# The last tile of a spectral filter, its buffers, its issue order, and the first row blocks behind it

## The chip, the cores and the metric

The kernel runs on one NeuronCore of one Trainium2 chip. The metric is the device time of one execution in microseconds (us); the smaller it is the better. The engines are named as the profile names them: PE (matrix multiply), PEld (its weight loads), DVE (VectorE), ACT (ScalarE), POOL (GpSimd) and SP, which here does nothing but issue DMAs.

## What is computed

A layer of two residual branches on x, 2048 rows of 512 float32 values:

```
h  = x + irfft2( rfft2(layernorm(x)) * (w_r + 1j*w_i) )
h2 = h + ( gelu(layernorm(h) @ w_gate) * (layernorm(h) @ w_up) ) @ w_down
```

w_gate and w_up are 512x1376, w_down is 1376x512. All outputs are float32.

## The kernel before

The Fourier transforms are matrix multiplications, folded by symmetry. **First stage**: 16 row blocks of 128 rows are transformed along the rows. **Filter stage** (the loop over `SECOND`): 16 tiles t. For each, `over_d` (L411) transforms along d (matmul L416, copied by ACT, L420), and `filtered` (L422) finishes the forward transform on PE (L427), multiplies by the weights on DVE (three products, L433 to L435, into t1 and t2) and adds z = t1 + t2 (L438) with a two-column patch behind it (L440): on POOL for tiles 0 to 14, on DVE for tile 15. `back` (L442) takes z back on PE (L448, two halves e of two matmuls each) and ACT copies the bank into gh (L450). z has 7 buffers. A tile is written into all 16 row blocks of gh, so no row block can be begun before the last tile is copied.

**Row blocks** (the list `FIRST`): for block b, `U` takes it back along d with four matmuls (`over_d_back`, L510, matmul L515), `C` copies the bank by ACT (L830), `V` adds its halves on DVE (L838) and `X` subtracts them on POOL (L866) into the two halves of one row `v`, `M` multiplies `v` by `mis` on PE (L848), `O`, `H`, `G` and `I` undo the symmetry and add x; the rest of the list normalizes the blocks and begins the gated layer. The remaining time, some 300 us, is the gated layer on PE.

The weights of the gated layer are split into a rounded part and a rest by `load_gu`: a weight tile lands in `raw`, **which has one buffer**; POOL makes sums of it (L138 to L146); then, for the first two weight tiles, seven pairs follow of a rounding on ACT (L93) and a subtraction on POOL (L94). The generator is advanced by one step at each `h` in `SECOND`; the steps cover weight tiles 0 and 1. In `FIRST`, `r0` is the first POOL step (L138) of weight tile 2, whose DMA into `raw` (L131, L132) can start when the last L94 of weight tile 1 has read the buffer.

Both lists are written out by hand, and the engines PE, ACT, DVE and POOL get their instructions in the order of the lists; each engine works strictly in its order. In `SECOND`, `o3.0` is `over_d` of tile 3 into bank 0, `f3` is `filtered`, `b3` is `back`, `p3` patches the weights of tile 3 on ACT (L453), and `h` is a step of the weight split. The loads of x for row blocks 0, 1, 4 and 5 go into `a` (L783), memory that the filter stage's buffers held before; SP too works in order.

Of the kernel before, what the change touches and what calls it, by code (L numbers as in the profile page):

```python
# [12 lines left out]
F32 = mybir.dt.float32  # L13
F32R = mybir.dt.float32r
I32 = mybir.dt.int32
AF = mybir.ActivationFunctionType
ALU = mybir.AluOpType
# [3 lines left out]
P = 128  # L21
NB = 16
NT = 16
NF = 11
NQ = 260
# [6 lines left out]
BY_THEN = (8, 12, 9)  # L32

FIRST = """
U4.0 C4.0 r0 U0.1 C0.1 U1.2 U5.3 V4.2 X4 V0.3 C1.4 V1.0 C5.5 X0 M4.1 V5.1 X1 O4.0 X5 M0.2 H4 U2.3 O0.1 G4 I4
M5.1 C2.5 H0 V2.3 G0 S4 U7.2 M1.3 O5.0 A4 U6.0 I0 U3.4 X2 H5 C7.1 S0 O1.1 A0 H1 M2.1 C6.0 Q0 C3.5 E0.5 N0 G5
U12.3 R01 V7.4 I5 T01.2 G1 I1 V6.3 S5 X7 A5 R00 T00 S1 O2.1 M7.0 X6 s0.0 A1 a0 Q1 l0 V3.1 E1.6 c0 d0 f0 b0 U8.4
U9.7 N1 e0.1 m0 g0 H2 h0 R10 k0 T10 R11 H7 n0 T11.1 X3 a1 s1.2 b1 c1 i0 d1 j0 l1 M3.2 C8 S7 g0aP0 o0 M6.4 e1.0
# [8 lines left out]
"""  # L47

SECOND = """
p0 p1 p2 h o0.0 h o1.6 o2.2 f0 o3.0 f1 p3 o4.2 f2 p4 h o5.0 o6.2 h f3 o7.0 h h p5 h f4 o8.2 p6 f5 b0 p7 b1 f6 o9.2 h h  # L50
h f7 p8 p9 b2 b3 o10.2 p10 f8 b4 h p11 o11.2 p12 f9 b5 o12.2 h h f10 b6 f11 o13.2 p13 b7 f12 h h o14.2 b8 f13 p14 o15.2
h f14 p15 b9 b10 h f15 b11 h b12 b13 b14 b15
"""
AHEAD = 8

# [2 lines left out]
def kernel(  # L58
# [16 lines left out]
    pe, act, dve, pool = nc.tensor, nc.scalar, nc.vector, nc.gpsimd  # L75
    x3 = x.rearrange("(p b) d -> p b d", b=NB)
    o3 = out.rearrange("(p b) d -> p b d", b=NB)

    base = ctx.enter_context(tc.tile_pool(name="base", bufs=1))
    gh = base.tile([P, NB, D], F32, name="gh")  # L80
# [25 lines left out]
    ps = ctx.enter_context(tc.tile_pool(name="ps", bufs=1, space=PSUM)).tile([P, 8, 512], F32, name="ps")  # L106
# [55 lines left out]
    with (  # L162
# [245 lines left out]
        w2 = ctx2.enter_context(tc.tile_pool(name="w2", bufs=2, reuse_waits="tile"))  # L408
        dps, zs = {}, {}
# [12 lines left out]
        def filtered(t):  # L422
            dp, wt = dps.pop(t), wts.pop(t)
            px = ps[:, 4 + 2 * (t % 2) : 6 + 2 * (t % 2), :NQ]
            for g in range(2):
                r = dp[:, g].rearrange("p e q -> p (e q)")
                pe.matmul(px[:, g], cfs[:, min(t, 1), g], r, start=True, stop=True)  # L427

            t1 = w2.tile([P, 2, NQ], F32, name="t1", bufs=3)
            t2 = w2.tile([P, 2, NQ], F32, name="t2", bufs=3)  # L430
            z = w2.tile([P, 2, NQ], F32, name="z", bufs=7)
            re, im = slice(0, 64), slice(64, P)
            dve.tensor_tensor(t1, px, wt[:, 0], op=ALU.mult)  # L433
            dve.scalar_tensor_tensor(t2[re], px[im], -1.0, wt[im, 1], op0=ALU.mult, op1=ALU.mult)
            dve.tensor_tensor(t2[im], px[re], wt[re, 1], op=ALU.mult)  # L435

            eng = dve if t == NT - 1 else pool
            eng.tensor_tensor(z, t1, t2, op=ALU.add)  # L438
            zs[t] = z
            eng.tensor_tensor(z[:, :, 0], z[:, :, 0], z[:, :, 128], op=ALU.add)  # L440

        def back(t):  # L442
            z = zs.pop(t)
            pg = ps[:, t % 2].rearrange("p (c g n) -> p c g n", c=4, g=2)
            for e in range(2):
                for g in range(2):
                    o, zg = pg[:, 2 * e : 2 * e + 2, g], z[:, g, 130 * e : 130 * e + P]
                    pe.matmul(o, zg, cis[:, min(t, 1), g], start=True, stop=True)  # L448
            ghv = gh.rearrange("p b (c t k) -> p t c b k", c=8, k=4)[:, t]
            act.activation(ghv, ps[:, t % 2].rearrange("p (c b k) -> p c b k", c=8, k=4), AF.Copy)  # L450

        def patch_w(t):
            act.activation(wts[t][:, :, :, 0:129:128], wh[:, t], AF.Copy)  # L453
# [2 lines left out]
        with tc.manual_schedule(engines={et.PE, et.Activation, et.DVE, et.Pool}):  # L456
            prep = itertools.chain(raw0, load_gu(1, True))
            for m, op in enumerate((ALU.add, ALU.subtract)):
                pool.tensor_tensor(wh[:, :, m], ws[:, 0, :, m], ws[:, 1, :, m], op=op)
            with tc.issue_after(kept.ins):  # L460
                act.activation(wh, wh, AF.Copy, scale=0.5)
            for _ in range(4):
                next(prep)
            rounded = 0
            for op in SECOND.split():
                name, *place = op.split(".")
                t = int(name[1:] or 0)
                if name == "h":
                    for _ in range(2 if rounded == 6 else 1):
                        next(prep, None)  # L470
                    rounded += 1
                elif name[0] == "o":
                    over_d(t, int(place[0]))
                elif name[0] == "f":
                    filtered(t)
                    if t + AHEAD < NT:
                        load_w(t + AHEAD)
                    if t == NT - 1:
                        for k, b in enumerate(BY_PE):
                            act.activation(nis[:, k], mis[:, b], AF.Copy, scale=-1.0)  # L480
                else:
                    (patch_w if name[0] == "p" else back)(t)
# [19 lines left out]
    def stats2(b):  # L502

        bn = w3.tile([P, 32], F32, name="bn")[:, :6]
        dve.bn_stats(bn, gh[:, b])
        yield
        dve.bn_aggr(mv2[:, b], bn)
        yield

    def over_d_back(b, bank):  # L510

        g = gh[:, b].rearrange("p (c k) -> p c k", c=4)
        pv = ps[:, bank].rearrange("p (e s n) -> p e s n", e=2, s=2)
        for c in range(4):
            pe.matmul(pv[:, c // 2, (c + c // 2) % 2], g[:, c], dis[:, c], start=True, stop=True)  # L515

    def norm_scales(b, n):
# [269 lines left out]
    do = {}  # L787
# [5 lines left out]
    def early(b):  # L793

        where = []

        def back(k):
            where.append(k)
            over_d_back(b, k)

        do[f"U{b}"] = back
        do[f"C{b}"] = lambda: act.activation(gh[:, b], ps[:, where[0]], AF.Copy)
        do[f"K{b}"] = lambda k: unfolded(b, rows[k])
# [9 lines left out]

    def whole(b):

        pv = sv = v = py = od = None
        xt, by_pe = sources[b], b in BY_PE

        def parts(a):
            return a.rearrange("p (e s n) -> p e s n", e=2, s=2)  # L820

        def back(k):
            nonlocal pv
            pv = ps[:, k]
            over_d_back(b, k)

        def keep(k):
            nonlocal sv
            sv = parts(rows[k])
            act.activation(rows[k], pv, AF.Copy)  # L830

        def unfold(k):
            nonlocal v
            v = rows[k]
            if b in BY_POOL:
                pool.tensor_tensor(parts(v)[:, :, 0], sv[:, :, 0], sv[:, :, 1], op=ALU.add)
            else:
                dve.tensor_tensor(parts(v)[:, :, 0], parts(pv)[:, :, 0], sv[:, :, 1], op=ALU.add)  # L838

        def back_s(k):  # L840
            nonlocal py
            py = ps[:, k].rearrange("p (e n) -> p e n", e=2)
            if by_pe:
                for e, m in enumerate((mis[:, b], nis[:, BY_PE.index(b)])):
                    pe.matmul(py[:, e], mis[:, b], v[:, :256], start=True, stop=False)
                    pe.matmul(py[:, e], m, v[:, 256:], start=False, stop=True)
            else:
                pe.matmul(ps[:, k], mis[:, b], v, start=True, stop=True)  # L848

        def odd(k):  # L850
            nonlocal od
            od = ods[k]
            act.activation(od, py[:, 1], AF.Copy)

        def residual():
            x2 = xt.rearrange("p (e n) -> p e n", e=2)
            y = py if by_pe else py[:, 0:1].to_broadcast([P, 2, 256])
            to = gh[:, b].rearrange("p (e n) -> p e n", e=2) if by_pe else x2
            dve.scalar_tensor_tensor(to, x2, mv[:, b, 0:1], y, op0=ALU.subtract, op1=ALU.add)

        def unfold2(e, op):
            x2, h2 = (a.rearrange("p (e n) -> p e n", e=2) for a in (xt, gh[:, b]))
            return lambda: pool.tensor_tensor(h2[:, e], x2[:, e], od, op=op)

        do[f"U{b}"], do[f"C{b}"], do[f"V{b}"], do[f"M{b}"] = back, keep, unfold, back_s
        do[f"X{b}"] = lambda: pool.tensor_tensor(parts(v)[:, :, 1], sv[:, :, 0], sv[:, :, 1], op=ALU.subtract)  # L866
        do[f"O{b}"], do[f"H{b}"] = odd, residual
        do[f"G{b}"], do[f"I{b}"] = unfold2(0, ALU.add), unfold2(1, ALU.subtract)
        st = stats2(b)
        do[f"S{b}"] = do[f"A{b}"] = lambda: next(st)  # L870
# [43 lines left out]
    for b in range(8):  # L914
        whole(b)
# [62 lines left out]
    with tc.manual_schedule(engines={et.PE}):  # L978
        for n, (q, f) in list(enumerate(tiles))[2:]:
            k, at_change = n - q * NF, n == NF - 1  # L980
# [175 lines left out]
```

## Time and profile before

| | us |
|---|---|
| median of 3 runs | 457.14 (456.63 to 457.20) |
| profiled execution, whole | 456.41 |
| profiled execution, span of the profile | 454.6 |
| PE busy | 438.9 (97% of the span) |
| first stage ends, filter stage begins (first L416) | 33.43 |
| last tile's copy (L450) ends, row blocks begin (first L515) | 78.06 |
| first M (L848) begins | 81.74 |

The profile is of one execution; its instructions carry source lines, so the stages can be told apart by line. The time line gives start and duration of each instruction or run of equal instructions; the chain of waits follows the end of the program back from each instruction to what released it. A busy PE says little alone: what counts are the places where it is idle and what ended that idle time.

### The profile page before, as it was taken

To read this page: it belongs to the slowest core of one execution; us is meant where nothing else is said; L and a number is where in the kernel's file an instruction comes from. 1 tells how busy PE (TensorE), PEld (TensorE's weight loads), DVE (VectorE), ACT (ScalarE), POOL (GpSimd) and SP (SyncE) were. 2 spreads that over 40 slices of the span, in tenths; PEclk is the share of its full clock that TensorE was granted. 3 is DMA by queue.
4 is the path that set the end of the run, shared out by engine and by line. 5 is a ranking of instruction groups with operands and counts; after the bars stand their busy time and mean duration, and the time that the engine had idled before them with its cause. 6 is when DMAs were issued, how large, how long until landed. Compare 5 with 4: busy or idle time off the path is not lost.

```text
span 454.6 us, 6435 instructions
## 1 busy us (share of the span) xinstructions
PE 438.9 (97%) x2289; PEld 371.4 (82%) x2289; DVE 276.9 (61%) x513; ACT 206.6 (45%) x433; POOL 275.5 (61%) x305
## 2 busy tenths in 40 slices
PE   3999998999999999999999999999999999999997
PEld 3899998788967777887888888888888888888876
DVE  5966986797665676358744579256565355535453
ACT  3979876688751233024422776242243024302420
POOL 5985996968868578828752744155566536663210
PEclk9999999999999999999999999999999999999999
DMA  8994804300031122112210203131022102210013
GB/s 253 399 406 132 284 32 156 123 25 1 25 115 47 48 92 92 48 47 71 69 46 25 70 25 128 57 85 55 25 70 69 48 24 71 69 46 25 23 66 121
DMA packets 21168, 41.05 MB, mean 90 GB/s; under 512 B 2064, under 2 KB 7696, under 8 KB 21008
## 3 DMA queue, kind: packets, MB, share of 16 engines
q1 hardware_dynamic: 21136, 40.64, 26.2%
q8 instruction: 18, 0.29, 0.3%
q14 instruction: 14, 0.11, 0.1%
HBM read 36.44 MB, written 4.19 MB: 89 GB/s over the span
## 4 chain that ended last, share of the span: by engine, by line
PE 89%; ACT 4%; DVE 2%; DMA 2%; issue 1%; SPq 1%; DVEq 0%; ACTq 0%
PE ps L747 26%; PE ps L100 15%; PE ps L102 15%; PE ps L101 15%; PE ps L416 3%; PE ps L515 3%; PE ps L427 3%; PE ps L448 2%; PE ps L288 2%; DMA gh<-in_x 2%; PE ps L848 1%; PE ps L956 1%; PE ps L554 1%; ACT ts L293 1%; PE ps L548 1%
## 5 line engine op out<-in xcount | busy, mean ns | idle before, releaser
L100 PE MATMUL ps<-cb,gu 128*128 128x512 f32 (+1 forms) x336 | 127.8, 380 | 2.0 <-ACT s L651 1.6
L747 PE MATMUL ps<-wd,a 128*128 128x512 f32 (+1 forms) x537 | 126.1, 388 | 0.2 <-DVE gh L750 0.2
L102 PE MATMUL ps<-cb,gu 128*128 128x512 f32 (+1 forms) x336 | 124.9, 372 | 0.0
L101 PE MATMUL ps<-cb,gu 128*128 128x512 f32 (+1 forms) x336 | 124.8, 371 | 0.0
L747 PEld LDWEIGHTS ps<-wd,a 128*128 128x128 f32 x537 | 99.2, 188 | 22.4 <-DVE gh L957 0.9
L156 POOL TENSOR_TENSOR gu<-raw,gu 128x768 fp32r<-128x768 f32 (+1 forms) x54 | 78.2, 1476 | 40.0 <-DVE gu L153 38.7
L651 ACT ACTIVATE s<-ps 128x512 f32<-128x512 f32 (+1 forms) x72 | 40.4, 561 | 134.4 <-PE ps L102 134.2
L100 PEld LDWEIGHTS ps<-cb,gu 128*128 128x128 f32 x336 | 63.2, 188 | 15.0 <-ACT s L651 2.2
L101 PEld LDWEIGHTS ps<-cb,gu 128*128 128x128 f32 x336 | 63.2, 188 | 11.7 <-issue 1.0
L102 PEld LDWEIGHTS ps<-cb,gu 128*128 128x128 f32 x336 | 63.2, 188 | 11.1
L753 DVE TENSOR_TENSOR gh<-ps,gh 128x512 f32<-128x512 f32 x48 | 33.0, 690 | 53.5 <-PE ps L747 53.4
L496 POOL TENSOR_TENSOR wd<-wdr,wd 128x512 fp32r<-128x512 f32 x22 | 28.5, 1295 | 51.5 <-ACT wd L494 51.5
L660 DVE TENSOR_TENSOR ps<-ps,s 128x512 f32<-128x512 f32 (+1 forms) x48 | 31.0, 649 | 24.8 <-PE ps L102 22.5
L666 ACT ACTIVATE a<-ps 128x512 fp32r<-128x512 f32 (+1 forms) x48 | 26.9, 561 | 39.0 <-DVE ps L660 38.6
L673 DVE TENSOR_TENSOR a<-ps,a 128x512 fp32r<-128x512 f32 (+1 forms) x48 | 30.7, 640 | 11.8 <-ACT a L666 10.4
L138 POOL TENSOR_TENSOR raw<-raw 128x256 f32<-128x256 f32 x20 | 14.7, 737 | 37.8 <-DMA raw<-in_wgu 36.7
L654 DVE TENSOR_TENSOR s<-ps,s 128x512 f32<-128x512 f32 (+1 forms) x48 | 30.8, 642 | 10.3 <-PE ps L102 8.7
L657 ACT ACTIVATE s<-s 128x512 f32<-128x512 f32 (+1 forms) x48 | 28.2, 592 | 18.4 <-DVE s L654 18.4
L654 DVE TENSOR_TENSOR ps<-ps,s 128x512 f32<-128x512 f32 (+1 forms) x24 | 15.7, 654 | 27.7 <-ACT s L651 27.7
L288 PE MATMUL ps<-ms,pn 128*128 128x128 f32 x120 | 17.6, 297 | 8.3 <-ACT ms L256 8.1
L288 PEld LDWEIGHTS ps<-ms,pn 128*128 128x128 f32 x120 | 16.1, 210 | 8.8 <-POOL pn L263 8.8
L153 DVE CAST gu<-raw 128x1792 fp32r<-128x1792 f32 x18 | 19.6, 1091 | 4.5 <-PE ps L101 2.9
(124 smaller groups left out, 609.7 us busy)
## 6 DMA issues: line engine op xcount, KB each, us to landing
raw<-in_wgu SPq DMA_DIRECT2D x40, 256.0 KB, 3.1
wt<-in_w SPq DMA_DIRECT2D x16, 520.0 KB, 5.4
wdr<-in_wd SPq DMA_DIRECT2D x22, 256.0 KB, 2.6
out<-gh SPq DMA_DIRECT2D x15, 256.0 KB, 2.0
gh<-in_x SPq DMA_DIRECT2D x7, 512.0 KB, 9.6
row<-in_x SPq DMA_DIRECT2D x12, 256.0 KB, 3.0
mis<-in_mi SPq DMA_DIRECT2D x1, 1024.0 KB, 10.7
a<-in_x SPq DMA_DIRECT2D x4, 256.0 KB, 4.3
```

The lines of the kernel that those rows point to most:

```text
L100: pe.matmul(o, lh, rh, start=(i == 0 and not onto), stop=False, skip_group_check=True)
L101: pe.matmul(o, lh, rl, start=False, stop=False, skip_group_check=True)
L102: last = pe.matmul(o, ll, rh, start=False, stop=(i == n - 1), skip_group_check=True)
L156: pooled["lo"] = pool.tensor_tensor(r[:, 1, m], t[:, m], r[:, 0, m].bitcast(F32), op=ALU.subtract)
L288: pe.matmul(pt[:, c], o, mc, start=(z == 0), stop=(z == len(parts[b][c]) - 1))
L496: pool.tensor_tensor(r[:, 1], t, r[:, 0].bitcast(F32), op=ALU.subtract)
L651: return lambda: act.activation(to, a, AF.Copy)
L654: return lambda: dve.tensor_tensor(to, a, b, op=ALU.add)
L660: return lambda: dve.tensor_tensor(u, u, g, op=ALU.mult)
L673: dve.tensor_tensor(a[:, 1], u, a[:, 0].bitcast(F32), op=ALU.subtract)
L747: pe.matmul(o, parts_of[tiles.index((q, f))][:, ha, i // 4, r], wds[f][:, hw, c], start=start, stop=stop)
L753: dve.tensor_tensor(gh[:, b, c], o, gh[:, b, c], op=ALU.add)
```

## The change

Four things are changed. (1) The sum z of tile 15 is split by columns: DVE adds columns 0 to 129 of each half and patches them, POOL adds columns 130 to 259. (2) The copy of tile 15 into gh is split: the matmuls of its second half e write bank 3, ACT copies the first half, DVE the second. (3) z gets 14 buffers. (4) `SECOND` is in a new order, and `FIRST` begins row blocks 4 and 0 by halves of d: `u4` and `u0` do the two matmuls that need the first half of gh, `w4` and `w0` the other two.

```diff
 FIRST = """
-U4.0 C4.0 r0 U0.1 C0.1 U1.2 U5.3 V4.2 X4 V0.3 C1.4 V1.0 C5.5 X0 M4.1 V5.1 X1 O4.0 X5 M0.2 H4 U2.3 O0.1 G4 I4
+u4.0 u0.1 w4 C4.0 r0 w0 C0.1 U1.2 U5.3 V4.2 X4 V0.3 C1.4 V1.0 C5.5 X0 M4.1 V5.1 X1 O4.0 X5 M0.2 H4 U2.3 O0.1 G4 I4
...
 SECOND = """
...
-h f14 p15 b9 b10 h f15 b11 h b12 b13 b14 b15
+f14 p15 h b9 b10 f15 h h b11 b12 h b13 b14 h b15
...
-            z = w2.tile([P, 2, NQ], F32, name="z", bufs=7)
+            z = w2.tile([P, 2, NQ], F32, name="z", bufs=14)
...
+            zs[t] = z
+            first = slice(0, NQ)
+            if t == NT - 1:
+                first, second = slice(0, 130), slice(130, NQ)
+                pool.tensor_tensor(z[:, :, second], t1[:, :, second], t2[:, :, second], op=ALU.add)
             eng = dve if t == NT - 1 else pool
-            eng.tensor_tensor(z, t1, t2, op=ALU.add)
-            zs[t] = z
+            eng.tensor_tensor(z[:, :, first], t1[:, :, first], t2[:, :, first], op=ALU.add)
             eng.tensor_tensor(z[:, :, 0], z[:, :, 0], z[:, :, 128], op=ALU.add)
 
         def back(t):
-            z = zs.pop(t)
-            pg = ps[:, t % 2].rearrange("p (c g n) -> p c g n", c=4, g=2)
+            z, last = zs.pop(t), t == NT - 1
+            ghv = gh.rearrange("p b (c t k) -> p t c b k", c=8, k=4)[:, t]
             for e in range(2):
+                pt = ps[:, 3 if last and e else t % 2]
+                pg = pt.rearrange("p (c g n) -> p c g n", c=4, g=2)
                 for g in range(2):
                     o, zg = pg[:, 2 * e : 2 * e + 2, g], z[:, g, 130 * e : 130 * e + P]
                     pe.matmul(o, zg, cis[:, min(t, 1), g], start=True, stop=True)
-            ghv = gh.rearrange("p b (c t k) -> p t c b k", c=8, k=4)[:, t]
-            act.activation(ghv, ps[:, t % 2].rearrange("p (c b k) -> p c b k", c=8, k=4), AF.Copy)
+                c = slice(4 * e, 4 * e + 4) if last else slice(0, 8)
+                if last and e:
+                    dve.tensor_copy(ghv[:, c], pt.rearrange("p (c b k) -> p c b k", c=8, k=4)[:, c])
+                elif last or e:
+                    act.activation(ghv[:, c], pt.rearrange("p (c b k) -> p c b k", c=8, k=4)[:, c], AF.Copy)
...
-    def over_d_back(b, bank):
+    def over_d_back(b, bank, cs=range(4)):
...
-        for c in range(4):
+        for c in cs:
...
+        def back_first(k):
+            nonlocal pv, bank
+            pv, bank = ps[:, k], k
+            over_d_back(b, k, (0, 1))
...
+        do[f"u{b}"], do[f"w{b}"] = back_first, lambda: over_d_back(b, bank, (2, 3))
```

What the new order does to an engine shows in its instructions as built. Behind the change the lines of the filter stage are 5 to 9 higher (L438 is L443, L440 is L444, L448 is L454, L450 is L459), and those of the row blocks 9 to 16 (L515 is L524, L783 is L792, L848 is L862, L866 is L881). POOL at the end of the filter stage, before, from the patch of tile 13 on (z_814 is tile 14, raw_575 weight tile 1, raw_913 weight tile 2, and row_889 the row `v` of block 4):

```order
L440 TENSOR_TENSOR z_794<-z_794 128x2
L94 TENSOR_TENSOR gu_82<-raw_575,gu_82 128x256
L438 TENSOR_TENSOR z_814<-t1_812,t2_813 128x520
L440 TENSOR_TENSOR z_814<-z_814 128x2
L94 TENSOR_TENSOR gu_82<-raw_575,gu_82 128x256 x2
L138 TENSOR_TENSOR raw_913<-raw_913 128x256
L866 TENSOR_TENSOR row_889<-row_887 128x2x128
```

The same place of the change (z_808 is tile 14, z_831 tile 15, raw_625 weight tile 1, raw_915 weight tile 2, row_891 the row `v` of block 4):

```order
L444 TENSOR_TENSOR z_789<-z_789 128x2
L94 TENSOR_TENSOR gu_82<-raw_625,gu_82 128x256
L443 TENSOR_TENSOR z_808<-t1_806,t2_807 128x520
L444 TENSOR_TENSOR z_808<-z_808 128x2
L94 TENSOR_TENSOR gu_82<-raw_625,gu_82 128x256
L441 TENSOR_TENSOR z_831<-t1_829,t2_830 128x2x130
L94 TENSOR_TENSOR gu_82<-raw_625,gu_82 128x256 x4
L138 TENSOR_TENSOR raw_915<-raw_915 128x256
L881 TENSOR_TENSOR row_891<-row_889 128x2x128
```

Between tile 14's patch and the first POOL step on weight tile 2 stood two subtractions L94; now five stand there and half a sum z. SP before, from the last weight tile of the filter on:

```order
L202 DMA wt_653<-in_w 128x1040
L783 DMA row_893<-in_x 128x512
L783 DMA row_895<-in_x 128x512
L783 DMA row_894<-in_x 128x512
L783 DMA row_896<-in_x 128x512
L131 DMA raw_913<-in_wgu 128x512
L132 DMA raw_913<-in_wgu 128x2x256
L783 DMA a_884<-in_x 128x512 x4
L491 DMA wdr_1327<-in_wd 128x512
```

And SP in the change:

```order
L202 DMA wt_655<-in_w 128x1040
L792 DMA row_895<-in_x 128x512
L792 DMA row_897<-in_x 128x512
L792 DMA row_896<-in_x 128x512
L792 DMA row_898<-in_x 128x512
L792 DMA a_886<-in_x 128x512 x4
L131 DMA raw_915<-in_wgu 128x512
L132 DMA raw_915<-in_wgu 128x2x256
L500 DMA wdr_1329<-in_wd 128x512
```

The four loads of x into `a` were issued behind weight tile 2, and are now issued ahead of it.

More of the change, by code (lines that the diff above doesn't have):

```diff
@@ L49 @@
 SECOND = """
-p0 p1 p2 h o0.0 h o1.6 o2.2 f0 o3.0 f1 p3 o4.2 f2 p4 h o5.0 o6.2 h f3 o7.0 h h p5 h f4 o8.2 p6 f5 b0 p7 b1 f6 o9.2 h h
-h f7 p8 p9 b2 b3 o10.2 p10 f8 b4 h p11 o11.2 p12 f9 b5 o12.2 h h f10 b6 f11 o13.2 p13 b7 f12 h h o14.2 b8 f13 p14 o15.2
-h f14 p15 b9 b10 h f15 b11 h b12 b13 b14 b15
+p0 h p1 p2 o0.0 o1.6 o2.2 f0 o3.0 f1 p3 o4.2 h f2 o5.0 o6.2 f3 o7.0 p4 h h f4 p5 o8.2 b0 f5 b1 p6 p7 h o9.2 h h f6 b2
+f7 p8 o10.2 b3 b4 f8 o11.2 h h p9 b5 p10 f9 o12.2 h f10 p11 p12 b6 p13 h o13.2 f11 b7 f12 o14.2 b8 p14 h f13 o15.2 h
+f14 p15 h b9 b10 f15 h h b11 b12 h b13 b14 h b15
 """
@@ L814, in whole @@
     def whole(b):
-        pv = sv = v = py = od = None
+        pv = sv = v = py = od = bank = None
         xt, by_pe = sources[b], b in BY_PE
```

## The prediction

> **What bounds the kernel now.** I read the page first, for which engine the span belongs to.
>
> ```profile
> span 454.6 us, 6435 instructions
> PE 438.9 (97%) x2289; PEld 371.4 (82%) x2289; DVE 276.9 (61%) x513; ACT 206.6 (45%) x433; POOL 275.5 (61%) x305
> PE 89%; ACT 4%; DVE 2%; DMA 2%; issue 1%; SPq 1%; DVEq 0%; ACTq 0%
> ```
>
> PE is busy for 97% of the span and is 89% of the chain that ends last. The change adds no matmul and takes none away, so only PE's idle time can change. Next, busy time by stretches around the end of the filter stage (us first, then PE, PEld, DVE, ACT, POOL, clock, DMA share, GB/s).
>
> ```profile
> 71.00:76.00 5.00, 4.67 (x37) 4.32 (x36) 4.73 (x7) 3.67 (x9) 4.84 (x7) 1.00 0.35 125
> 76.00:82.00 6.00, 5.07 (x41) 4.84 (x42) 1.20 (x4) 2.76 (x6) 2.14 (x5) 1.00 0.79 268
> 82.00:98.00 16.00, 16.00 (x99) 12.71 (x97) 13.79 (x35) 12.11 (x27) 13.31 (x21) 1.00 0.15 49
> 98.00:135.00 37.00, 34.86 (x251) 30.89 (x249) 25.59 (x67) 26.88 (x66) 26.94 (x34) 1.00 0.13 43
> ```
>
> PE idles 0.33 us in the first stretch and 0.93 in the second, about 1.26 together, then not at all for 16 us, then 2.14 in 37 us. The first 1.26 us are the aim of the change. PE's time line from the last tile on, with what ended each idle time in brackets:
>
> ```profile
> 71.82 3.85 PE L448 MATMUL ps<-cis,z 128*128 128x128 f32 x32
> 76.25 1.13 PE L448 MATMUL ps<-cis,z 128*128 128x128 f32 x8 [0.57 <-DVE z L440]
> 78.06 3.84 PE L515 MATMUL ps<-dis,gh 128*128 128x128 f32 x32 [0.69 <-ACT gh L450]
> 81.74 1.88 PE L848 MATMUL ps<-row,mis 128*128 128x512 f32 x4
> ```
>
> PE waits 0.57 for the sum z of tile 15 and 0.69 for its copy; then 16 matmuls of row blocks (32 records) run to the first M (M4) at 81.74 without a gap. M4 reads the row whose halves V4 (DVE) and X4 (POOL) write. POOL and SP over the same time:
>
> ```profile
> 72.01 0.73 POOL L94 TENSOR_TENSOR gu<-raw,gu 128x256 fp32r<-128x256 f32 x1
> 72.70 1.29 POOL L438 TENSOR_TENSOR z<-t,t 128x520 f32<-128x520 f32 x1
> 74.07 0.20 POOL L440 TENSOR_TENSOR z<-z 128x2 f32<-128x2 f32 x1
> 74.22 1.86 POOL L94 TENSOR_TENSOR gu<-raw,gu 128x256 fp32r<-128x256 f32 x2
> 79.95 0.73 POOL L138 TENSOR_TENSOR raw<-raw 128x256 f32<-128x256 f32 x1 [3.86 <-DMA raw<-in_wgu]
> 80.63 2.79 POOL L866 TENSOR_TENSOR row<-row 128x256 f32<-128x256 f32 x4
> ```
>
> ```profile
> 76.11 0.33 SPq L131 DMA_DIRECT2D raw<-in_wgu  x1
> 76.48 0.44 SPq L132 DMA_DIRECT2D raw<-in_wgu  x1
> 77.02 1.82 SPq L783 DMA_DIRECT2D a<-in_x  x4
> ```
>
> This is a second path to M4, and the important one. The last L94 ends at 74.22 + 1.86 = 76.08 and frees the one `raw` buffer; SP issues the next weights at 76.11; POOL idles 3.86 us until they have landed, because L138 stands ahead of X4 in its order. X4, the first of the four at 80.63, ends at 80.63 + 0.73 = 81.36, only 0.38 us before M4.
>
> **The change, part by part.** *PE's tail.* The half copy on ACT and that on DVE have their nearest rows in copies and sums of 256 columns out of PSUM:
>
> ```profile
> 82.80 0.38 ACT L853 ACTIVATE od<-ps 128x256 f32<-128x256 f32 x1 [0.26 <-PE ps L848]
> 79.89 0.42 DVE L838 TENSOR_TENSOR row<-ps,row 128x256 f32<-128x256 f32 x1 [3.79 <-ACT row L830]
> 75.71 0.60 ACT L450 ACTIVATE gh<-ps 128x512 f32<-128x512 f32 x1 [0.30 <-PE ps L448]
> 73.41 0.41 ACT L93 ACTIVATE gu<-raw 128x256 fp32r<-128x256 f32 x1
> ```
>
> PE's matmuls of tile 14 end about 75.5 (71.82 + 3.85, less the 0.2 that the last one's end lies behind the next start). The half sums come by about 75.4 (below), so the 0.57 shrinks to about nothing. The first half of tile 15 is 4 of the 8 records and ends near 76.1. ACT copies tile 14 until 75.71 + 0.60 = 76.31, then has one L93 (0.41, now between tiles 14 and 15), then the half copy (0.38; between 0.3 and 0.6): 77.0. PE starts row block 4 about 77.05 instead of 78.06: 1.0 us gained. DVE's half copy is needed four matmuls later and is covered by them; without that cover it would cost some 0.4. PE would reach M4 at 81.74 - 1.0 = 80.7.
>
> *POOL's tail.* Now the other path.
>
> ```profile
> 71.33 0.69 DVE L435 TENSOR_TENSOR t<-ps,wt 64x520 f32<-64x520 f32 x1
> 74.34 1.16 DVE L438 TENSOR_TENSOR z<-t,t 128x520 f32<-128x520 f32 x1
> 48.26 2.10 POOL L94 TENSOR_TENSOR gu<-raw,gu 128x256 fp32r<-128x256 f32 x3
> ```
>
> Tile 14's products are ready at 71.33 + 0.69 = 72.02. Before, POOL took its sum only at 72.70, behind an L94 that had waited for its ACT half; that half now stands earlier in ACT's list, so the sum can start at 72.1 and the patch end at 72.1 + 1.29 + 0.08 + 0.20 = 73.67 instead of 74.27. Behind it stood two L94, now one L94, the half sum and four L94. Three L94 in a row take 2.10, so 0.70 each. The half sum, 128x260, is between the 0.70 of 256 columns and the 1.29 of 520; I take 0.70. DVE adds its half at the same moment, and here the trace shows the two holding each other up: DVE's whole sum takes 1.16 beside two L94, which take 1.86 instead of 1.40; it fits DVE waiting until the first L94 ends (74.94), then 0.56 alone. Half of that is about 0.3. So: 73.67 + 0.70 + 0.3 + 0.70 + 4 x 0.70 = 78.17, against 76.08. Bounds: 77.8 if the halves run side by side, 78.8 if tile 14 comes no earlier. Below that it can't be: tile 15's products end near 74.3 in either kernel, as PE's matmuls ahead of them are as many, and 0.70 + 4 x 0.70 lie behind them.
>
> The Trainium skill, "SBUF — State Buffer", section "SBUF: two separate sides", makes that last point a rule: a VectorE instruction with two inputs in SBUF and a GpSimd instruction that reads SBUF take a shared port pair by an exclusive lock, and the later one is fully blocked. By this rule the split sum is no parallel work at all, and the end is 78.17; without it, it would be 77.87. The trace agrees as far as it goes (1.16 and 1.86 above); no run yet shows two halves of one sum begun together.
>
> *From the freed buffer to M4.* Before, 79.95 - 76.08 = 3.87 us passed from the last L94 to L138. SP's two issues are in it, and the landing of the second:
>
> ```profile
> DMA to landing us min/median/max: 3.0/3.2/6.4
> ```
>
> That is L132, twenty times in this kernel; in this stretch it took 3.3. The four loads of x now go first; they wait for POOL's half sum (75.4) and take 1.82 to issue, so SP is free again at 77.2, ahead of 78.17, and the weights share the DMA engines with less. With 3.0 instead of 3.3 the path is 3.57; I take 3.72, between 3.57 and 3.87. L138 then starts at 81.89; X4 ends 81.36 - 79.95 = 1.41 later, at 83.30; M4 follows by the 0.1 to 0.2 of a wait and a weight load, at 83.48. C4, behind `w4` now, and V4 are done before 80, and the loads of x that H4 needs come earlier: both are off this path.
>
> *The sum.* M4 at 83.48 instead of 81.74 is **+1.7 us**; the bounds are 77.8 + 3.57 + 1.41 + 0.15 = 82.9 (+1.2) and 78.8 + 3.87 + 1.41 + 0.2 = 84.3 (+2.5). PE waits 83.5 - 80.7 = 2.8 there, and the 1.0 gained is lost inside that wait. All that follows in the list hangs on M4: PE executes in order, POOL's next three X and DVE's H4 stand behind it, so I let the whole rest move by 1.7.
>
> *Fourteen buffers.* POOL's waits ahead of its 15 sums:
>
> ```profile
> L438 POOL TENSOR_TENSOR z<-t,t 128x520 f32<-128x520 f32 x15 | 19.4, 1291 | 3.6 <-DVE t L435 3.1 <-PE ps L416 0.6
> ```
>
> At most 0.6 of 3.6 us are waits for PE, hence for a z buffer, and none is at the end of the stage: nothing gained, and their cost is only memory. The new order up to tile 13 gives PE the same matmuls, and it was never idle there (4.67 of 5.00 us is the last stretch); I put it at nothing, between -0.3 and +0.3.
>
> The profiled execution took 456.41 (454.6 of span and 1.8 around it) and becomes 458.1. The median of the runs is 457.14, 0.73 above the profiled one, so the forecast for it is 457.14 + 1.7 = 458.8.
>
> **The rivals.** *PE's tail decides (faster).* If X4 were ready by 80.7, the gain of 1.0 would stand: 457.14 - 1.0 = 456.1. For this the last L94 would have to end about 75.4 (80.7 less 0.15, 1.41 and 3.72), before tile 15's products allow POOL's half sum and four L94 to be done; it turns only on a misread order of POOL. Chance 0.07.
>
> *The delay is absorbed (no change).* M4 comes late, but between 98 and 135 us PE idles 2.14 us anyway; if these waits end on something that M4 doesn't move, up to a good part of 1.7 is swallowed. At 0.9 or more swallowed the time is 457.1 to 458.0, say 457.7. Against it: before 98 there is no idle time at all, and what is waited for behind it (sums and copies of the same row blocks) comes from M4 on. Chance 0.17.
>
> *POOL becomes the bound of the row blocks (slower still).* POOL is late by 81.89 - 79.95 = 1.94, PE by 1.74, and POOL is busy 13.31 of the 16 us up to 98. If a later X or a G then ends a wait too, the rest moves by POOL's full delay, 2.0 to 2.5: 459.4. Slack of the later X against their M is larger than X4's 0.38, so 0.10.
>
> **How the numbers follow.** The forecast has 0.66, the rivals 0.07, 0.17 and 0.10. The range reaches from a largely absorbed delay (457.14 + 0.3) to the upper bound of the sum (457.14 + 2.5): 457.4 to 459.6. About 0.9 us, or 0.2%, is what a measurement of this kernel can tell from no change. Forecast and third rival are slower by more, the second rival is within it: slower 0.76, same 0.17, faster 0.07.
>
> **What would show it.** Right: five L94 behind tile 14's patch, the last ending near 78.2; an idle time of POOL of 3.5 to 3.9 us ahead of L138, ended by the DMA; PE starting row blocks near 77.0 but idling 2 to 3 us before the first L862, ended by POOL's L881. Wrong: no idle time of PE before that L862, or a landing much under 3 us; or PE's idle time between 98 and 135 falling well below 2.1, which would mean that the delay was swallowed.

## The result and the profile after

The change takes **461.28 us** (median of 6 runs, 459.98 to 463.92) against 456.88 (6 runs, 456.38 to 457.36) of the kernel before on the same chip: the ratio is 1.0102 [1.0076, 1.0129], 4.4 us slower. The profiled execution took 461.33, its span is 459.6. The forecast was +1.7 us, 458.8; the time lies above the range of 457.4 to 459.6.

The page first: span, busy times and the chain that ended last.

```profile
span 459.6 us, 6438 instructions
PE 439.8 (96%) x2289; PEld 372.4 (81%) x2289; DVE 277.4 (60%) x514; ACT 205.8 (45%) x433; POOL 276.4 (60%) x306
PE 87%; DVE 3%; DMA 3%; POOL 2%; ACT 2%; issue 1%; SPq 0%; DVEq 0%; POOLq 0%; ACTq 0%
```

PE does the same 2289 pieces in 0.9 us more and is idle for some 4 us more, and POOL has come into the chain. What PE waited for up to 140 us (total, times, longest):

```profile
PE ps L288 <- ACT ms L256: 9.7, 2, 7.2
PE ps L862 <- POOL row L881: 3.5, 1, 3.5
PE ps L100 <- ACT s L660: 1.6, 3, 0.7
PE ps L416 <- ACT ts L293: 0.7, 1, 0.7
PE ps L524 <- ACT gh L459: 0.3, 1, 0.3
```

The second row is the wait that was forecast. The last one is what is left of the two idle times, 0.57 and 0.69, at which the change aims. PE's time line, first the start of the filter stage, then its end:

```profile
34.66 2.95 PE L416 MATMUL ps<-dfs,ts 128*128 128x130 f32 x24 [0.69 <-ACT ts L293]
...
78.07 3.84 PE L524 MATMUL ps<-dis,gh 128*128 128x128 f32 x32 [0.27 <-ACT gh L459]
85.45 3.56 PE L862 MATMUL ps<-row,mis 128*128 128x512 f32 x4 [3.55 <-POOL row L881]
```

The filter stage began at 34.66 in this execution and at 33.43 in that of before, though the change touches nothing of the first stage; so the two are compared by times **counted from the first L416**. The row blocks begin 43.41 us behind it instead of 44.63, 1.22 us earlier. The first M (L862) begins 50.79 behind it instead of 48.31, 2.48 later. It also takes 3.56 us where the same four records took 1.88. POOL and SP in the same stretch:

```profile
74.66 0.20 POOL L444 TENSOR_TENSOR z<-z 128x2 f32<-128x2 f32 x1
74.81 0.73 POOL L94 TENSOR_TENSOR gu<-raw,gu 128x256 fp32r<-128x256 f32 x1
75.58 0.92 POOL L441 TENSOR_TENSOR z<-t,t 128x260 f32<-128x260 f32 x1
76.46 2.78 POOL L94 TENSOR_TENSOR gu<-raw,gu 128x256 fp32r<-128x256 f32 x4
84.00 0.72 POOL L138 TENSOR_TENSOR raw<-raw 128x256 f32<-128x256 f32 x1 [4.76 <-DMA raw<-in_wgu]
84.68 1.41 POOL L881 TENSOR_TENSOR row<-row 128x256 f32<-128x256 f32 x2
```

```profile
76.52 1.75 SPq L792 DMA_DIRECT2D a<-in_x  x4
79.26 0.33 SPq L131 DMA_DIRECT2D raw<-in_wgu  x1
79.63 0.43 SPq L132 DMA_DIRECT2D raw<-in_wgu  x1
```

Behind tile 14's patch stand five L94 and half a sum, as the order says, and the last L94 ends at 79.24. Then POOL idles for 4.76 us, where before it was 3.86: the weights, issued at once, land later, and the four loads of x stand right ahead of them. The landing time of L132 here, by the view of that line:

```profile
DMA to landing us min/median/max: 4.2/4.2/4.2
```

In the kernel before it was 3.3. Last, the same 16 us behind the end of the stage that were shown of before, and the next 37 (us, then busy time of PE, PEld, DVE, ACT and POOL, clock, DMA share, GB/s):

```profile
82.00:98.00 16.00, 12.55 (x64) 9.08 (x65) 9.01 (x23) 7.62 (x17) 11.87 (x17) 0.89 0.16 51
98.00:135.00 37.00, 34.91 (x265) 32.15 (x264) 26.95 (x70) 28.35 (x69) 29.50 (x37) 1.00 0.07 19
```

Before, PE was busy for all 16 us and the granted clock was 1.00. Now it is idle for 3.45 us and the clock is 0.89. From 98 on it idles 2.09 us against 2.14, and 2.13 in the 37 us that begin 5.1 us later, as the work does by then: nothing of the delay is swallowed there. The clock's 0.89 is not spread over the stretch. Cut where the clock changes:

```profile
81.83:85.25 3.42, 0.07 (x1) 0.00 (x0) 0.00 (x0) 0.60 (x1) 1.25 (x2) 1.00 0.48 159
85.25:88.66 3.41, 3.21 (x4) 1.51 (x5) 1.53 (x3) 0.38 (x1) 2.20 (x4) 0.50 0.02 5
88.66:98.00 9.34, 9.34 (x61) 7.57 (x60) 7.49 (x21) 6.70 (x15) 8.41 (x12) 1.00 0.11 32
```

For 3.41 us behind the wait, PE ran at half its clock. Two theories, then. **A**, the forecast's chain with a longer landing: five L94 and SP's new order make weight tile 2 late, `r0` (L138) stands ahead of X4 on POOL, and PE waits for X4; the halved clock follows from that wait. **B**, the rival: the split pieces and the halved row blocks themselves cost time on PE or POOL, or the clock falls for a reason of its own, and the wait for the weights only takes the place of others.

### The profile page after: what moved, and what is told of

Same layout as the page of the kernel before. It is cut to its first block, busy times and chain, and to the rows that moved or that the text cites. A ratio compares the mean times of both kernels' runs of the same rounds, so it can differ in the third digit from the quotient of the medians.

```text
span 459.6 us, 6438 instructions
## 1 busy us (share of the span) xinstructions
PE 439.8 (96%) x2289; PEld 372.4 (81%) x2289; DVE 277.4 (60%) x514; ACT 205.8 (45%) x433; POOL 276.4 (60%) x306
## 4 chain that ended last, share of the span: by engine, by line
PE 87%; DVE 3%; DMA 3%; POOL 2%; ACT 2%; issue 1%; SPq 0%; DVEq 0%; POOLq 0%; ACTq 0%
PE ps L756 26%; PE ps L100 15%; PE ps L101 15%; PE ps L102 15%; PE ps L288 4%; PE ps L416 2%; PE ps L524 2%; PE ps L427 2%; DMA gh<-in_x 2%; PE ps L862 2%; PE ps L454 1%; PE ps L971 1%; POOL gu L94 1%; DMA raw<-in_wgu 1%; POOL z L443 1%
## 5 line engine op out<-in xcount | busy, mean ns | idle before, releaser
L138 POOL TENSOR_TENSOR raw<-raw 128x256 f32<-128x256 f32 x20 | 14.8, 738 | 38.2 <-DMA raw<-in_wgu 37.1
L443 POOL TENSOR_TENSOR z<-t,t 128x520 f32<-128x520 f32 x15 | 19.5, 1297 | 7.2 <-DVE t L435 6.6
```

## The experiments

Times of experiments are medians beside runs of the kernel before on the same chip: 457.30 us (30 runs, 455.84 to 460.15) for the first four, 457.22 (32 runs, 456.00 to 460.10) for the next four, 456.20 (23 runs, 455.69 to 458.06) for the last two. The three groups ran on three chips, so kernels of different groups are better compared by their ratios than by their medians.

### The change with the old filter order

```diff
-p0 h p1 p2 o0.0 o1.6 o2.2 f0 o3.0 f1 p3 o4.2 h f2 o5.0 o6.2 f3 o7.0 p4 h h f4 p5 o8.2 b0 f5 b1 p6 p7 h o9.2 h h f6 b2
+p0 p1 p2 h o0.0 h o1.6 o2.2 f0 o3.0 f1 p3 o4.2 f2 p4 h o5.0 o6.2 h f3 o7.0 h h p5 h f4 o8.2 p6 f5 b0 p7 b1 f6 o9.2 h h
...
```

> The change with the old SECOND list; everything else of the change stays. Theory A (the loss is the wait of the first M for X4, which stands on POOL behind L138 and so behind the landing of the weights in the one raw buffer, and the halved clock that follows this idle time): two L94 and the half sum stand behind tile 14 again, the last L94 ends near 76.5, X4 is ready at 81.4 to 82, the idle time of PE ahead of the first L862 is under 1.5 us, no halved clock follows; 456.3 to 457.5. Theory B (the loss comes from the split sum, the split copy, the begun blocks or the memory of the 14 buffers): 460 to 461.5, as the whole change.

Measured: 457.43 us (12 runs), ratio 1.0007 [0.9989, 1.0026]. PE and POOL:

```profile
75.57 2.09 PE L454 MATMUL ps<-cis,z 128*128 128x128 f32 x16 [1.07 <-POOL z L444]
77.69 3.84 PE L524 MATMUL ps<-dis,gh 128*128 128x128 f32 x32
83.73 1.98 PE L862 MATMUL ps<-row,mis 128*128 128x512 f32 x4 [2.20 <-POOL row L881]
```

```profile
56.81 0.73 POOL L138 TENSOR_TENSOR raw<-raw 128x256 f32<-128x256 f32 x1 [2.13 <-DMA raw<-in_wgu]
...
76.85 0.73 POOL L94 TENSOR_TENSOR gu<-raw,gu 128x256 fp32r<-128x256 f32 x1
82.27 0.72 POOL L138 TENSOR_TENSOR raw<-raw 128x256 f32<-128x256 f32 x1 [4.69 <-DMA raw<-in_wgu]
```

Without the new order the loss is gone. The profiled execution (458.17, above the median) is no good picture of why: PE's wait at the first M, 2.20, is more than the 1.5 us that I expected at most. POOL ran late in it: its sum of tile 14 began 40.76 us behind the first L416 (at 33.14), against 39.55 in the last kernel below, which has the same order there. The first row of POOL shows where that began: weight tile 1 (L138 of it) was waited for 2.13 us, against 0.73 in the kernel before and 0.90 in the last kernel below, and POOL had no other long wait from there to tile 14. So PE waited 1.07 us for tile 14, and the last L94 ended 44.44 behind the first L416, about as late as in the change. The weights of tile 2 then took 4.69 us though they were issued ahead of the loads of x; the issue of L132 alone lasted 1.48 us instead of 0.43. What stretched it stays open. The clock stayed whole after these 2.20 us of idle time.

### The new filter order alone, in the kernel before

The same lines of `SECOND` the other way round, in the kernel before, with its seven z buffers and its whole pieces.

> The kernel before with the new SECOND list alone (7 buffers, whole sum on DVE, whole copy, whole first blocks). Theory A: five L94 behind tile 14, the last ending 78 to 79; PE idles 2 to 3 us ahead of the first M, where POOL's X4 ends the wait, and the clock is halved for one window of 3.4 us behind it; 459.5 to 461.5. Theory B: within 0.5 us of before.

Measured: 460.79 us (12 runs), ratio 1.0067 [1.0044, 1.0090]. POOL and PE:

```profile
74.64 3.92 POOL L94 TENSOR_TENSOR gu<-raw,gu 128x256 fp32r<-128x256 f32 x5
83.55 0.72 POOL L138 TENSOR_TENSOR raw<-raw 128x256 f32<-128x256 f32 x1 [4.99 <-DMA raw<-in_wgu]
```

```profile
72.69 5.12 PE L448 MATMUL ps<-cis,z 128*128 128x128 f32 x40
78.49 3.84 PE L515 MATMUL ps<-dis,gh 128*128 128x128 f32 x32 [0.69 <-ACT gh L450]
85.01 3.42 PE L848 MATMUL ps<-row,mis 128*128 128x512 f32 x4 [2.68 <-POOL row L866]
```

The order by itself brings the five L94, 4.99 us of waiting for the weights, PE's wait and the four records of 3.42 at half clock. Most of the loss is here, without any split piece. The order also takes away the 0.57 us that PE waited for the sum of tile 15, though that sum is whole here: DVE's sum began at 75.20, when the first of the five L94 was nearly over, and took 0.72 us. In the kernel before it began 0.12 us behind an L94 and took 1.16.

### The first POOL step on weight tile 2 moved behind the first row block

```diff
-u4.0 u0.1 w4 C4.0 r0 w0 C0.1 U1.2 U5.3 V4.2 X4 V0.3 C1.4 V1.0 C5.5 X0 M4.1 V5.1 X1 O4.0 X5 M0.2 H4 U2.3 O0.1 G4 I4
+u4.0 u0.1 w4 C4.0 w0 C0.1 U1.2 U5.3 V4.2 X4 V0.3 C1.4 V1.0 C5.5 X0 M4.1 V5.1 X1 O4.0 X5 M0.2 H4 U2.3 O0.1 G4 I4 r0
```

> The change with r0 (L138, the first POOL step on weight tile 2) moved in FIRST from behind C4 to behind I4, so that X4, X0, X1, X5, G4 and I4 go ahead of it. Theory A: X4 follows C4 at once, PE reaches the first L862 without a wait of more than 0.3 us, the clock stays, and the tail's 1.0 us is kept: 455.5 to 456.3. Theory B (PE waits for something else once X4 is out of the way, or POOL's later work is what counts): 458 or more.

Measured: **455.51 us** (7 runs, 455.21 to 455.66), ratio 0.9952 [0.9931, 0.9974]: faster than the kernel before. PE, then POOL:

```profile
77.18 3.84 PE L524 MATMUL ps<-dis,gh 128*128 128x128 f32 x32 [0.28 <-ACT gh L459]
80.86 1.88 PE L862 MATMUL ps<-row,mis 128*128 128x512 f32 x4
```

```profile
75.57 2.78 POOL L94 TENSOR_TENSOR gu<-raw,gu 128x256 fp32r<-128x256 f32 x4
79.50 2.12 POOL L881 TENSOR_TENSOR row<-row 128x256 f32<-128x256 f32 x3 [1.15 <-ACT row L844]
...
84.53 0.74 POOL L138 TENSOR_TENSOR raw<-raw 128x256 f32<-128x256 f32 x1
```

The five L94 and the late weights are all still there (L132 took 4.3 us to land); only X4 no longer stands behind them. PE goes from the row blocks into the first M without a gap, L138 finds its weights ready, and the clock is whole. Against the change this is some 6 to 7 us less (5.8 by the medians, 6.9 by the ratios). It settles A for the wait: of what the change costs nothing is left once `r0` no longer stands ahead of X4.

### The wait filled with matmuls

Fourteen matmuls into an unused bank are added ahead of the first M; nothing reads them.

```diff
-... C5.5 X0 M4.1 ...
+... C5.5 X0 zz M4.1 ...
...
+        for _ in range(14):
+            pe.matmul(ps[:, 7, :P], ident, dis[:, 0], start=True, stop=True)
```

> The change with 14 more matmuls of 128x128 (3.1 us on PE, into a bank that nothing reads) ahead of the first M, where PE idles 3.5 us. They use no time that PE had a use for. If the halved clock for 3.4 us is the answer to this idle time (theory A's second half), it goes and the time falls by 1.2 to 1.7 against the change: 459 to 460. If the clock drops for another reason, or its drop costs nothing, the time stays at 460.5 to 461.5 or rises.

Measured: 459.80 us (12 runs), ratio 1.0038 [1.0019, 1.0057].

```profile
81.70 3.29 PE L957 MATMUL ps<-dis,ident 128*128 128x128 f32 x28
85.94 1.98 PE L862 MATMUL ps<-row,mis 128*128 128x512 f32 x4 [0.94 <-POOL row L881]
```

The M comes no earlier (POOL's weights landed even later, 5.29 us of idle time there), but PE runs it in 1.98 instead of 3.56 us, and the median is 1.5 us below that of the change. In this execution the halved clock at that place is gone with PE's idle time, while the late load and the instructions are still there. The runs agree: all six of the change have a mean clock of 0.996 or less, down to 0.988, and none of these twelve is below 0.995. Nine of them still stand at 0.995 or 0.996; in the profiled one this is a window in the first stage, and where it lies in the others no trace shows.

### The kernel before, with that step moved

The same move of `r0` as above, in the kernel before.

> The kernel before with r0 alone moved behind I4; nothing of the change. If X4's wait for the weights costs the kernel before something too in many of its executions (its slack was 0.38 us and the landing varies), then the time falls to 456.2 to 456.8 and its spread under 1 us, with PE's idle time of 1.26 us at the tail still there. If the gain of the change with r0 late comes from the split tail alone, the time stays at the 457.3 of before.

Measured: 457.83 us (12 runs, 456.13 to 460.45), ratio 1.0011 [0.9990, 1.0033]. No gain in the median; in the profiled execution of the kernel before X4 was ready ahead of its M anyway. That needn't hold for each execution: in the one profiled here the issue of L132 lasted 1.54 us and the weights landed 4.4 us behind its start, at 81.3. With `r0` ahead of it X4 would have ended about 1.4 us behind that, at 82.7, while the M began at 81.65 (an estimate, from the 1.41 us between the start of L138 and the end of X4 in the kernel before). I had expected the spread of the runs to shrink, and it didn't: the runs with a mean clock of 1.000 lie at 456.1 to 456.7, but for one at 458.5, and those at 0.992 to 0.996 at 457.8 to 460.5. Most of the spread here goes with the clock. Not all of it does: runs of the kernel before with a clock of 0.999 or more reach 457.9 on this chip and 460.1 on that of the first four experiments, and why stays open.

### The weights issued ahead of the loads of x

SP issues weight tile 2, and one load of w_down, ahead of the four loads into `a`, in the change: the generator of weight tile 2 is begun earlier, and the four loads wait until its second load is issued.

```diff
-        nc.sync.dma_start(t[:, 3:6:2], wgu[f, :, 2:])
+        pooled["in"] = nc.sync.dma_start(t[:, 3:6:2], wgu[f, :, 2:])
...
+    raw2 = load_gu(2)
+    next(raw2)
...
-        nc.sync.dma_start(sources[b], x3[:, b])
+        with held("in") if b % 4 < 2 else ExitStack():
+            nc.sync.dma_start(sources[b], x3[:, b])
```

> The change with the DMAs of weight tile 2 (and one of w_down) issued by SP ahead of the four loads of x into a, as in the kernel before; POOL's order is that of the change. If the four loads ahead made the weights land late (4.2 us for the second DMA, against 3.3 before), the second DMA lands in 3.0 to 3.6, POOL idles 3.5 to 4.0 us ahead of L138 instead of 4.8, and the first M comes 0.7 to 1.1 us earlier against the end of POOL's last L94; the time falls by 0.3 to 1.5, less if the x loads are then late. If the landing varies for other reasons, it stays at 3.9 to 4.5 and the time at 460.5 to 461.5.

Measured: 459.36 us (9 runs), ratio 1.0049 [1.0032, 1.0066].

```profile
76.61 2.77 POOL L94 TENSOR_TENSOR gu<-raw,gu 128x256 fp32r<-128x256 f32 x4
83.25 0.72 POOL L138 TENSOR_TENSOR raw<-raw 128x256 f32<-128x256 f32 x1 [3.87 <-DMA raw<-in_wgu]
```

```profile
84.71 1.98 PE L865 MATMUL ps<-row,mis 128*128 128x512 f32 x4 [2.65 <-POOL row L884]
```

POOL's wait is back at 3.87, as in the kernel before, 0.89 shorter than in the change. L132 took 3.3 us to land. So the loads of x ahead of the weights are what made them late: in the seven profiles with the loads ahead L132 took 4.2 to 4.7 us, and 3.2 or 3.3 in the three with the weights ahead and an issue of 0.43 us. In the other two with the weights ahead, where the issue itself lasted 1.48 and 1.54, it took 4.1 and 4.4 from the start of the issue. The time fell by 1.9 us against the change, more than the 0.3 to 1.5 that I expected. PE still waits 2.65 us, as the five L94 remain, but here the clock stayed whole at that place, where 2.68 us had halved it in the order alone. The section on the clock comes back to this.

### The sum whole, the copy whole

Two kernels, each the version with `r0` late and one split taken back: tile 15's sum whole on DVE, or its copy whole on ACT (with blocks 4 and 0 begun whole).

```diff
-            if t == NT - 1:
-                first, second = slice(0, 130), slice(130, NQ)
-                pool.tensor_tensor(z[:, :, second], t1[:, :, second], t2[:, :, second], op=ALU.add)
```

> The change with r0 late and with tile 15's sum whole on DVE again. If the two halves hold each other up at the shared operands (0.43 and 0.92 in the trace of the change), the split gains little: z is ready 0.1 to 0.4 us later, and the time rises by 0 to 0.4 over the 455.5 of r0 late. If the halves ran side by side, the whole sum costs 0.5 or more.

```diff
-                pt = ps[:, 3 if last and e else t % 2]
+                pt = ps[:, t % 2]
...
-                if last and e:
-                    dve.tensor_copy(ghv[:, c], pt.rearrange("p (c b k) -> p c b k", c=8, k=4)[:, c])
-                elif last or e:
-                    act.activation(ghv[:, c], pt.rearrange("p (c b k) -> p c b k", c=8, k=4)[:, c], AF.Copy)
+                if e:
+                    act.activation(ghv, pt.rearrange("p (c b k) -> p c b k", c=8, k=4), AF.Copy)
```

> The change with r0 late, with tile 15's copy whole on ACT and the blocks 4 and 0 begun whole. By the sum of the prediction the split copy saves the second half of tile 15's matmuls (0.45) and half of the copy (0.2): PE starts the row blocks 0.5 to 0.8 us later, and the time is 456.0 to 456.3. If the first M is bound by something else by then, the time stays at 455.5.

Measured: 455.95 us with the sum whole (12 runs), ratio 0.9979 [0.9960, 0.9997], and 455.82 with the copy whole (12 runs), ratio 0.9974 [0.9961, 0.9987]. The intervals overlap with each other and with that of the version with both splits. The traces tell more, counted from the first L416 (34.17 and 33.97 there):

```profile
77.58 3.84 PE L521 MATMUL ps<-dis,gh 128*128 128x128 f32 x32
```

```profile
77.78 3.84 PE L521 MATMUL ps<-dis,gh 128*128 128x128 f32 x32 [0.69 <-ACT gh L456]
```

The first row, of the whole sum, is 43.41 us behind it, as with both splits (43.40): splitting the sum brings nothing. The second, of the whole copy, is 43.81 behind it: splitting the copy brings 0.4 us, less than the 0.5 to 0.8 that I expected, and the 0.69 of idle time that the kernel before had is back.

### Seven z buffers, and the old order, with that step late

Two more kernels on the version with `r0` late: z with seven buffers, and `SECOND` as before the change.

> The version with r0 behind I4 (455.51 us), its z buffers back at seven instead of fourteen. Theory: in the new order no tile's sum is made more than seven tiles ahead of its inverse transform, or where it is POOL has the time to wait, so the buffers are worth nothing: 455.3 to 456.0 us, row blocks beginning 43.4 us behind the first matmul of L416, as with fourteen. Rival: the new order runs DVE and POOL further ahead, so that seven buffers make POOL's sum (L443 or L444) wait for PE's reading of an old z, and the sums of tiles 14 and 15 come later: row blocks 0.5 us or more later and 456.0 to 457.5 us. Bound between the two: an interval against the fourteen-buffer version's ratio of 0.9952.

> The version with r0 behind I4 (455.51 us), the filter stage's order back as it was in the kernel before. Theory: the split sum and copy of tile 15 gain nothing in the old order, because there PE waits 1.07 us for tile 14's patched sum of POOL (L444) ahead of its last tiles, as the change with the old order showed; row blocks then begin 44.6 us behind the first matmul of L416 (43.4 with the new order) and the time is 1.2 us above it, 456.4 to 457.0 us, ratio 0.998 to 1.000. Rival: the new order is worth nothing here and the split and the late r0 do it all: 455.3 to 455.9 us.

Measured: seven buffers 455.22 us (12 runs, 454.49 to 455.98), ratio 0.9967 [0.9954, 0.9980]; the old order 455.97 (12 runs, 454.49 to 459.20), ratio 1.0005 [0.9982, 1.0027]. The start of the row blocks in the two:

```profile
77.10 3.84 PE L524 MATMUL ps<-dis,gh 128*128 128x128 f32 x32 [0.25 <-ACT gh L459]
```

```profile
76.31 3.84 PE L524 MATMUL ps<-dis,gh 128*128 128x128 f32 x32
```

With first L416 at 33.69 and 32.73 they are 43.41 and 43.58 us behind it. Seven buffers are enough, and this version and the one with fourteen are faster than both the kernel before and the change. For the old order my theory had said 44.6, and the profiled execution shows the rival: hardly a wait for tile 14, and 0.2 us of difference. Yet its median is 0.75 above the other's. Four runs at 458 to 459 make part of that, three of them with a mean clock of 0.991 to 0.996; the other eight have a median of 455.67, still above 455.22. In the earlier kernel with the old order DVE's half sum began 0.16 us behind POOL's sum of tile 14 and took 1.41 us (74.06 to 75.47); here POOL's sum (72.28 to 73.57) was over before it began, and it took 0.43. Such a collision in some executions could make the rest of the difference; it is argued, not shown, and what the new order is worth once `r0` is late stays open.

## When the clock is halved

In all twelve profiles the granted clock changes only at whole multiples of 3.413 us, counted from its first record, which comes 10 to 13 us into the span. So I counted PE's busy time in the windows of that grid, from there on. The window ahead of the halved one in the order alone, the window with most of the wait in the old order, and the two windows across which the wait lies with the weights first:

```profile
81.12:84.53 3.41, 1.21 (x11) 1.02 (x10) 0.42 (x1) 1.25 (x3) 0.98 (x2) 1.00 0.56 193
```

```profile
79.97:83.39 3.42, 1.56 (x14) 1.37 (x13) 0.84 (x2) 1.64 (x3) 1.12 (x2) 1.00 0.88 291
```

```profile
79.65:83.06 3.41, 2.41 (x22) 2.21 (x20) 0.85 (x2) 2.28 (x4) 0.00 (x0) 1.00 0.72 221
83.06:86.48 3.42, 1.77 (x4) 0.86 (x5) 1.04 (x3) 0.38 (x1) 3.23 (x5) 1.00 0.67 240
```

With 1.21 us of work in a window (in the change 0.07) the next one has half the clock; with 1.56, 1.77 or 2.41 it has not. So 2.65 us of waiting, cut in two by the grid, cost nothing more, and 2.68 us that lay mostly in one window cost about 1.5: from the first M to the first L845 it is 11.44 us in the order alone, 9.91 in the kernel before and 9.73 (L862) with the weights first. The first stage gives the other cases. The window ahead of a halved one in the change, and the emptiest window there that had no such effect, in the kernel with the whole copy:

```profile
10.15:13.57 3.42, 1.39 (x12) 1.20 (x11) 2.71 (x11) 2.92 (x9) 3.42 (x4) 1.00 1.02 416
```

```profile
12.18:15.59 3.41, 1.82 (x16) 1.64 (x16) 3.24 (x11) 3.11 (x11) 3.41 (x3) 1.00 1.02 418
```

Over all profiles the limit lies between 1.40 (the first stage with the weights first) and 1.56 us of PE work in 3.41. In each of these halving windows PE also had 2.0 us or more of idle time in one piece, and in the others 1.85 at most; which of the two counts, these windows can't tell. The Trainium skill, "TensorE: Matmul & The Clock Gate", Part 1, says that the gate looks at a free-running window of 4096 cycles, 3413 ns; the trace agrees. It puts the half rate behind an idle window; here windows in which PE was 35 to 41% busy were enough.

How a wait falls on the grid differs from run to run. Three of the twelve runs of the order alone have a mean clock of 1.000 and took 458.6 to 459.2 us; the four at 0.996 took 459.7 to 460.9, the four at 0.993 461.5 to 462.1, and the one at 0.989 463.3. One halved window makes 0.004 of the mean clock (half of 3.41 us in 457).

In the first stage PE waits for loads and statistics, and where these waits fall on the grid differs between the profiles. Three of the twelve profiles have a halved window there (the change, the filled wait, the weights first). The kernel before probably has it in some runs too: its mean clock is 0.992 to 0.996 in 25 of the 85 runs beside the experiments, though none of these left a trace.

## Why the prediction was wrong

- **"The new order up to tile 13 ... at nothing", "Fourteen buffers ... nothing gained".** Right for the buffers; what the order moves at its end was counted elsewhere in the sum, and is most of the loss (the order alone: 460.79 us).
- **PE's tail: row blocks 1.0 us earlier.** The gain came, 1.22, but not as told. The sum counted on the half sums to take away the wait of 0.57; the order does it alone, with a whole sum: its row blocks begin 44.09 behind the first L416 (78.49, with L416 at 34.40), 0.54 earlier than before. Everything else together brings 0.68 more; of that the split copy is worth 0.4 and the split sum nothing, and the rest belongs to no part that was taken back alone. As forecast, the gain is lost inside the wait.
- **POOL's tail: the last L94 later by 2.09 (78.17 against 76.08).** Right: counted from the first L416, 44.58 against 42.65, later by 1.93. The half sum took 0.92, against 0.70 + 0.3. DVE's half took 0.43, and POOL's alone (with the old order) 0.74, so POOL was held up by about 0.2.
- **"From the freed buffer to M4": 3.72, because the weights "share the DMA engines with less".** Wrong, and this is the first step that failed. The part of it up to L138 took 4.76. The loads of x were issued from 76.52 and took 2.8 to 4.3 us to land, so they were still on the engines when the weights came at 79.26; that SP itself was free again was no help. Weights first gave 3.87. The term was too small by 1.04.
- **The sum +1.7 at the first M.** 1.74, less 0.16 (last L94), plus 1.04 (landing), less 0.14 (from L138 to M 1.45 instead of 1.59) is 2.48, and 2.48 is what the trace shows.
- **"I let the whole rest move by" the same.** Wrong, the second step that failed, and a term that the sum lacked. It goes back to the first paragraph, "only PE's idle time can change": PE was busy for 0.9 us more with the same pieces, at a lower clock. PE's wait of 3.55 us emptied a window of the clock, and the next 3.41 us ran at half clock. At the first M the trace is late by 3.71 us, and by 5.11 where L845 (now L859) begins, 96.76 against 91.65: 1.40 more. Filling the wait took 1.5 off the time.
- **The two executions' first stages.** 1.23 us of the 5.0 between the spans was there before the filter stage began, and isn't the change's: 5.0 - 1.2 = 3.8. The medians differ by 4.4; four of the six runs of the change have a mean clock of 0.993 or less, as much as two halved windows make, so probably one beside that at the wait, against 25 of 85 runs of before with one or two. Whether that is more than chance six runs can't tell.
- **Absorbed** was wrong (2.09 against 2.14 us of idle time from 98 to 135), **POOL the bound of the row blocks** too: no later L862 waits for an L881.

## What to carry to other kernels

When a list is reordered, follow the queue of every engine that it touches up to the next buffer it frees: here three more subtractions and half a sum slid behind the last whole sum of a stage, freed the one weight buffer later, and an unrelated step that waited for it held up the critical one; moving that one step made 455.5 us of 461.3. A DMA that leaves earlier isn't free if something urgent is issued behind it, since it is in the way until it has landed. And a PE wait of two microseconds or more (3.41 less the 1.40 that were too little) may cost more than its length, because the clock behind it may be halved for a window.

## What was not expected of the hardware

- The clock follows PE's work in fixed windows of 3.413 us: 1.40 us of work or less halved the next window, 1.56 or more did not. What a wait costs so depends on how it lies on the grid (2.65 us: nothing more; 2.68 us: about 1.5).
- The second load of a weight tile (L132) took 3.2 or 3.3 us to land when it was ahead of the four loads of x, 256 KB each, and 4.2 to 4.7 when these were issued in the three microseconds or so before it. Twice it was ahead and took 4.1 and 4.4, with an issue that lasted 1.5 us instead of 0.43.
- DVE's sum of 260 columns took 0.43 us when it began ahead of POOL's, which then took 0.92 instead of 0.74; begun 0.16 us behind a sum of 520 columns on POOL, it took 1.41. "SBUF — State Buffer" of the Trainium skill, section "SBUF: two separate sides", has the one that comes later blocked for the whole instruction; the time of 1.41 agrees roughly (it ended 0.30 us behind POOL's sum, less than its own 0.43), while POOL lost 0.18 us, less than the 0.32 that DVE's sum still ran when POOL's began.
